# Attention with 16 queries a head: outputs of 15 blocks kept in SBUF and stored by one DMA, and an empty first pass through TensorE's program

## The chip, the core and the metric

The kernel runs on one core of a Trainium2 chip. The metric is the device time of one execution in microseconds (us), as the median of several runs. Shorter is better.

## The reference

```python
B, H, Sq, Skv, Dh = 8, 16, 16, 2048, 256

def reference(q, k, v):
    scale = q.shape[-1] ** -0.5
    scores = jnp.einsum('bhqd,bhkd->bhqk', q, k) * scale
    attn = _softmax(scores, axis=-1)
    return jnp.einsum('bhqk,bhkd->bhqd', attn, v)
```

All is bf16. There are 128 heads (8 x 16), each with 16 queries, 2048 keys and values, and 256 numbers a row. K and V are 134 MB each, q and the output 1 MB each, so the core has to read some 269 MB.

## The kernel before

Eight heads make a block, since 8 heads x 16 queries fill 128 partitions. There are G = 16 blocks (numbers 0 to 15, `last` = 15). Per block 8 MB of K and 8 MB of V are read; a DMA takes 4 MB of K (half a block) or 8 MB of V (a whole block), with 64 to 128 rows of 512 bytes lying one behind the other in each partition. `SL` holds them: two K slots (`KA`, `KB`) and one V window of two slots (`VW`).

What is done with a block:

- VectorE transposes K in place, in 32 x 32 squares (`kt`, line 196).
- TensorE multiplies queries by K into `S_ps` (`qk`, lines 309 and 310).
- VectorE takes the negated maximum (line 220), ScalarE the exponentials and their sums (line 292), VectorE transposes these (lines 229, 231), and both engines copy them into the sparse weights `PTz` (lines 203, 205, 277).
- TensorE multiplies the 128 weight tiles by the 128 V rows of a partition into `O_ps` (`pv`, line 332).
- ScalarE scales the sum by the inverse of the exponentials' sum and writes it as bf16 into the one output buffer `O_fin` (`evac`, line 271).

Each engine has its own program, and semaphores tie them. SyncE (`on_sync`) issues all loads. It waits before each K load until the scores of an earlier block are done (`c_qk`) and before each V load until the V rows that it overwrites have been used (`c_pv`). The V of the last two blocks comes in pieces (`PIECES`: 3 for block 14, 9 for block 15), so that the last ones are small. Behind them SyncE waits for the last eviction (`c_ev`) and stores block 15 (line 156).

ScalarE (`on_scalar`) stores the other 15 blocks from inside its loop: in the round of block g it evicts block g - 1, waits for the write to be done, and issues the store at line 301. Before an eviction it waits on `s_st`, which counts landed stores, since `O_fin` is used again. GpSimd presets the counts (line 161).

TensorE (`on_tensor`) waits for the first weights (`c_qw`), works on the scores of block 0 in small loops, and then has one loop over r from 1 to 16: scores of block r (left out for r = 16), some spare multiplications, and then `pv` for block r - 1, written out as 128 matmuls.

Of the kernel before, what the change touches and what calls it, by code (L numbers as in the profile page):

```python
# [4 lines left out]
ACTF = mybir.ActivationFunctionType  # L5
ALU = mybir.AluOpType
AX = mybir.AxisListType
PE = mybir.EngineType.PE
# [3 lines left out]
BF16 = mybir.dt.bfloat16  # L12
# [3 lines left out]
SPARE = 5  # L16
# [4 lines left out]
def bass_standalone__softmax_full_bidir__sampling_kernel(  # L21
# [16 lines left out]
    ku = k.rearrange("b h s d -> (b h s) d").rearrange("(u p t) d -> u p t d", p=128, t=T)  # L38
    vb = v.rearrange("b h s d -> (b h s) d").rearrange("(g p t) d -> g p t d", p=128, t=2 * T)
    qh = q.rearrange("b h s d -> (b h) (s d)")  # L40
    oh = out.rearrange("b h s d -> (b h s) d").rearrange("(g p) d -> g p d", p=128)

    with ExitStack() as es:
        ec = es.enter_context
# [8 lines left out]

        PTz = ec(nc.sbuf_tensor("PTz", [128, 2, T, 128], BF16))
        mk = ec(nc.sbuf_tensor("mk", [128, 1], F32))
        O_fin = ec(nc.sbuf_tensor("O_fin", [128, D], BF16))
        negm = ec(nc.sbuf_tensor("negm", [128, 1], F32))
        lsum = ec(nc.sbuf_tensor("lsum", [128, 2], F32))
        ltot = ec(nc.sbuf_tensor("ltot", [128, 1], F32))
# [69 lines left out]
        def on_sync(eng):  # L129
            def load_v(w, a, n):  # L130

                eng.wait_ge(c_pv, 8 * w + (a + n + C - 1) // C)
                eng.dma_start(VW[:, a:a + n, :], vb[w, :, a:a + n, :]).then_inc(s_p[w][a] if a else s_v, 16)  # L133

            eng.dma_start(QX, qh).then_inc(s_q, 16)  # L135
            for g, s0, s in ((0, VA, s_k0), (1, KA, s_k)):
                for e in range(2):
                    load_k(eng, g, e, s0 + e, 0, T, s[e])

            for e in range(2):  # L140
                eng.wait_ge(c_qk, 4 * e + 4)
                eng.dma_start(VW[:, T * e:T * e + T, :], vb[0, :, T * e:T * e + T, :]).then_inc(s_v0 if e else s_v, 16)
            with nc.Fori(2, last, engines=[SP]) as j:
                for e in range(2):
                    eng.wait_ge(c_qk, 8 * j + 4 * e - 4)
                    load_k(eng, j, e, KA + e, 0, T, s_k[e])
                load_v(j - 1, 0, 2 * T)
            for e in range(2):
                eng.wait_ge(c_qk, 8 * last + 4 * e - 4)
                load_k(eng, last, e, KA + e, 0, T // 2, s_k[e])  # L150
                load_k(eng, last, e, KA + e, T // 2, T // 2, s_kl[e])
            for w in PIECES:
                for a, n in PIECES[w]:
                    load_v(w, a, n)
            eng.wait_ge(c_ev, G + 1)
            eng.dma_start(oh[last], O_fin[:]).then_inc(s_fin, 16)
            eng.wait_ge(s_fin, 16)

        def on_gpsimd(eng):

            for x, n in ([(c_ev, 1), (c_ri, 2), (c_cp, 1), (c_pv, 8), (s_st, 17)] + [(x, 1) for x in s_kl] +
                         [(x, 1) for w in s_p for x in s_p[w].values()]):
                eng.sem_inc(x, n)
            zero = [PTz[:, e].rearrange("p t c -> p (t c)").bitcast(F32) for e in range(2)]
            eng.memset(zero[0], 0.0).then_inc(c_pool, 1)
            eng.wait_ge(c_qt, 2)
            for n in range(12):

                eng.wait_ge(c_cq if n else c_pool, max(n, 1))
                eng.tensor_copy(*qx(1 + n // 4, n % 4)).then_inc(c_cq, 1)  # L170

            eng.wait_ge(c_qt, 6)
            eng.wait_ge(c_qw, 4)
            eng.wait_ge(c_cq, 12)
            eng.memset(zero[1], 0.0).then_inc(c_pool, 1)
# [81 lines left out]
        def on_scalar(eng):  # L257
            def qwb(src):
                for a in range(4):
                    dv = QW[32 * a:32 * a + 32, :, 16 * a:16 * a + 64, :]  # L260
                    dv = bass.AP(tensor=dv.tensor, offset=QW[32 * a:32 * a + 32, 0, 16 * a, :].offset,
                                 ap=[list(dv.ap[0]), [1024 + 512, 2], [2, 64], [1, 2]])
                    eng.activation(dv, src(a), ACTF.Copy, scale=scale).then_inc(c_qw, 1)  # L263

            def evac(n, st):

                eng.wait_ge(c_pv, 8 * n)
                eng.wait_ge(c_ri, 2 * n)

                eng.wait_ge(s_st, st)  # L270
                eng.activation(O_fin[:], O_ps[:, 0:D], ACTF.Copy, scale=rinv[:, bass.ds(n, 1)]).then_inc(c_ev, 1)  # L271

            def copies(e, rs):
                for r in rs:
                    for x in range(2):
                        dst, src, m = weights(e, r, x)
                        eng.activation(dst, src, ACTF.Copy, scale=m if x else 1.0).then_inc(c_cp, 1)  # L277

            eng.wait_ge(c_qt, 2)
            qwb(lambda a: QXu[0:32, a, 0:2, :, :])  # L280
            eng.wait_ge(c_pool, 2)
            eng.wait_ge(c_qt, 6)
            eng.wait_ge(c_mk, 7)
            with nc.Fori(0, G, engines=[ACT]) as g:
                eng.wait_ge(c_qk, 8 * g + 8)
                qwb(lambda a: QTu[32 * a:32 * a + 32, bass.ds(((g + 1) & 15) * 2, 2), :, :])
                eng.wait_ge(c_mx, g + 1)
                for h in range(2):

                    sv = S_ps[:, 2 * h, :]  # L290
                    sv = bass.AP(tensor=sv.tensor, offset=sv.offset, ap=[list(sv.ap[0]), [32, 32], [1, 2], [2, 16]])
                    eng.activation(P_sb[:, 16 + 1024 * h:16 + 1024 * h + 1024], sv, ACTF.Exp,  # L292
                                   bias=negm[:], scale=1.0, accum_out=lsum[:, h:h + 1]).then_inc(c_ex[h], 1)
                eng.wait_ge(c_pt, 4 * g + 4)
                eng.wait_ge(c_pv, 8 * g + 4)
                copies(0, (0, 1))
                gg = eng.to_reg(g)
                with eng.If_ne(gg, 0):
                    evac(g + 1, 16 * g + 1)
                    eng.wait_ge(c_ev, g + 1)  # L300
                    eng.dma_start(oh[(g + 15) & 15], O_fin[:]).then_inc(s_st, 16)
                copies(1, (0, 1, 2))
            evac(G + 1, 16 * last + 17)

        def on_tensor(eng):
            def mm(dst, w, x, start, stop, load, check=True):
# [8 lines left out]
            def qk(e, cs, slot):  # L315
                for bp in range(8):
                    for c in cs:
                        ins = mm(S_ps[:, c, :], QW[:, e, :, bp], SLk[:, slot, c, bp // 2, bp % 2, :, :],
                                 e == 0 and bp == 0, e == 1 and bp == 7, c == cs[0])
                return ins  # L320
# [13 lines left out]
                    if t % C == C - 1:  # L334
                        ins.then_inc(c_pv, 1)

            eng.wait_ge(c_qw, 4)

            for c in range(4):
                if c == 0:  # L340
                    eng.wait_ge(c_pool, 1)
                mm(S_ps[:, c, :], PTz[:, 0, 0, :], PTz[:, 0, 0:4, :].rearrange("p t m -> p (t m)"), True, False, c == 0, False)
            with nc.Fori(0, 2, engines=[PE]) as e:
                for h in range(2):
                    with nc.Fori(0, 4, engines=[PE]) as b:
                        eng.wait_ge(c_kt, 2 * e + h + 1)
                        for par in range(2):
                            for c in (2 * h, 2 * h + 1):
                                ins = mm(S_ps[:, c, :], QW[:, e, :, 2 * b + par], SLk[:, VA + e, c, b, par, :, :],
                                         False, False, c == 2 * h, False)  # L350
                        if h:
                            ins.then_inc(c_qk, 1)

            with nc.Fori(1, G + 1, engines=[PE]) as r:
                rr = eng.to_reg(r)
                with eng.If_lt(rr, G):
                    for e in range(2):
                        for h in range(2):
                            eng.wait_ge(c_kt, 4 * r + 2 * e + h + 1)
                            if e + h == 0:  # L360
                                eng.wait_ge(c_ex[1], rr)
                            ins = qk(e, (2 * h, 2 * h + 1), KA + e)
                        ins.then_inc(c_qk, 4)

                    mid = eng.to_reg(((r + 14) & 16) + ((r + 1) & 16))
                    with eng.If_eq(mid, 16):
                        with nc.Fori(0, SPARE, engines=[PE]) as x:
                            for _ in range(4):
                                mm(X_ps[:], QW[:, 1, :, 7], QT[:, 0:512], True, True, False)
                lim = {last - 1: eng.to_reg(((r + 1) & 16) + 1), last: eng.to_reg((r & 16) + 1)}  # L370
                eng.wait_ge(c_ev, rr)
                eng.wait_ge(c_cp, 10 * r - 5)
                eng.wait_ge(c_cd, 6 * r - 2)
                eng.wait_ge(s_v, 16 * r)
                pv(lim)

        on_sync(nc.sync)
        on_gpsimd(nc.gpsimd)
# [31 lines left out]
```

## Time and profile before

| | |
|---|---|
| median of 3 runs | 634.5 us (634.5 to 634.57) |
| span of the profiled execution, first to last instruction | 633.1 us |
| HBM read, written | 269.48 MB, 1.05 MB |
| mean rate over the span | 427 GB/s |
| busy: PE, DVE, ACT | 539.1, 444.2, 241.8 us |
| store of one block by ScalarE, issue to landing | 23.5 us (7.9 to 23.9) |
| store of block 15 by SyncE, issue to landing | 1.5 us |

The profile describes one execution. Its own time outside the span isn't listed; 1.4 us lie between its span and the median of the runs. PE is TensorE's matmul, PEld its loading of weights, DVE is VectorE, ACT ScalarE, POOL GpSimd, SP SyncE; a q behind a name means that engine's sequencer. A window is a stretch of the span in us from its start. The DMA share is the mean busy share of the core's 16 DMA engines. Queue q1 carries what SyncE issues, q10 what ScalarE issues; q8 and q14 carry instructions that the engines fetch. In a chain of waits a line gives start, length and what was waited for; in a timeline the bracket at the end gives the idle time before an instruction and what ended it.

### The profile page before, as it was taken

The numbers are of one execution on the slowest core, as the hardware profiler recorded it, in microseconds if no ns is written. First come the engines' busy times: TensorE is split into PE (matmuls) and PEld (weight loads), VectorE is DVE, ScalarE is ACT, GpSimd is POOL, SyncE is SP. The second block draws the span as 40 slices with busy tenths as digits, with TensorE's granted clock in tenths as the row PEclk, the third lists the DMA queues.
The fourth block names the chain that finished last, engine by engine and source line by source line (L and its number), as shares of the span: only waits on it lengthen the run. The fifth ranks groups of instructions, "written<-read, shape, count | busy, mean of one in ns | idle before, by whom it ended". The sixth has DMA issues, their size and how long they took to land.

```text
span 633.1 us, 8100 instructions
## 1 busy us (share of the span) xinstructions
PE 539.1 (85%) x3336; PEld 273.3 (43%) x2561; DVE 444.2 (70%) x285; ACT 241.8 (38%) x309; POOL 21.5 (3%) x18
## 2 busy tenths in 40 slices
PE   1659989889898897989979899797989979899997
PEld 0112824518244272542725336263362724518386
DVE  5989794865948658496575966759567595769750
ACT  1027542622336233352424425244252442623453
POOL 7600000000000000000000000000000000000000
PEclk9998989999898999989999899999998999999999
DMA  8999999999999999999999999999999999999997
GB/s 366 433 433 437 434 443 424 452 411 441 437 428 436 430 433 461 405 459 406 458 413 425 438 427 437 455 404 460 406 462 409 427 437 429 435 420 428 432 427 297
DMA packets 11234, 270.56 MB, mean 427 GB/s; under 512 B 1248, under 2 KB 3552, under 8 KB 3936
## 3 DMA queue, kind: packets, MB, share of 16 engines
q1 hardware_dynamic: 9072, 269.55, 98.8%
q10 hardware_dynamic: 2160, 0.98, 0.5%
q8 instruction: 1, 0.02, 0.0%
q14 instruction: 1, 0.01, 0.0%
HBM read 269.48 MB, written 1.05 MB: 427 GB/s over the span
## 4 chain that ended last, share of the span: by engine, by line
DMA 57%; PE 32%; DVE 6%; issue 4%; SPq 0%; DVEq 0%; ACT 0%
DMA SL<-in_v_dram 45%; PE O_ps L332 30%; DMA SL<-in_k_dram 12%; DVE SL L196 4%; PE S_ps L309 1%; PE S_ps L310 1%; DVE PTz L203 0%; DVE PTb L231 0%; DVE negm L220 0%; DVE PTz L205 0%; DVE PTa L229 0%; SPq L127 0%; SPq L133 0%; ACT O_fin L271 0%; SPq L135 0%
## 5 line engine op out<-in xcount | busy, mean ns | idle before, releaser
L196 DVE STREAM_TRANSPOSE SL<-SL 128x4096 f32<-128x4096 f32 x64 | 282.3, 4433 | 81.7 <-DMA SL<-in_k_dram 80.8
L309 PE MATMUL S_ps<-SL,QW 128*128 128x512 bf16 (+1 forms) x512 | 206.3, 403 | 68.5 <-DVE SL L196 58.9
L332 PEld LDWEIGHTS O_ps<-SL,PTz 128*128 128x128 bf16 x2048 | 198.8, 98 | 103.0 <-DMA SL<-in_v_dram 79.2
L332 PE MATMUL O_ps<-SL,PTz 128*128 128x256 bf16 x2048 | 226.7, 273 | 13.5 <-DMA SL<-in_v_dram 12.4
L310 PE MATMUL S_ps<-SL,QW 128*128 128x512 bf16 (+1 forms) x512 | 204.8, 400 | 0.0
L309 PEld LDWEIGHTS S_ps<-SL,QW 128*128 128x128 bf16 (+1 forms) x512 | 74.3, 145 | 244.6 <-issue 155.2
L263 ACT ACTIVATE QW<-QT 32x256 bf16 x64 | 26.9, 420 | 202.5 <-PE S_ps L310 201.3
L277 ACT ACTIVATE PTz<-PTa 16x1024 bf16<-16x1024 bf16 x32 | 33.8, 1056 | 112.0 <-PE O_ps L332 100.2
L220 DVE TENSOR_REDUCE negm<-S_ps 128x1 f32<-128x2048 f32 x16 | 36.6, 2289 | 55.1 <-PE S_ps L310 55.1
L310 PE MATMUL X_ps<-QT,QW 128*128 128x512 bf16 x260 | 58.2, 379 | 0.0
L277 ACT ACTIVATE PTz<-PTb 16x1024 bf16<-16x1024 bf16 x48 | 50.6, 1055 | 10.9 <-ACT O_fin L271 10.1
L229 DVE STREAM_TRANSPOSE PTa<-P_sb 128x1024 bf16<-128x1024 bf16 x32 | 39.2, 1224 | 21.9 <-ACT P_sb L292 21.9
L277 ACT ACTIVATE PTz<-PTa,mk 32x1024 bf16<-32x1024 bf16 x48 | 54.3, 1130 | 0.0
L231 DVE STREAM_TRANSPOSE PTb<-P_sb 128x1024 bf16<-128x1024 bf16 (+1 forms) x32 | 39.0, 1218 | 0.0
L292 ACT ACTIVATE P_sb<-S_ps,negm 128x1024 bf16<-128x1024 f32 x32 | 35.4, 1110 | 5.9 <-DVE negm L220 5.9
L277 ACT ACTIVATE PTz<-PTb,mk 32x1024 bf16<-32x1024 bf16 x32 | 36.2, 1132 | 0.0
L271 ACT ACTIVATE O_fin<-O_ps,rinv 128x256 bf16<-128x256 f32 x16 | 7.6, 474 | 51.5 <-PE O_ps L332 51.5
L203 DVE TENSOR_SCALAR PTz<-PTb,mk 32x1024 bf16<-32x1024 bf16 x32 | 15.2, 476 | 0.0
L205 DVE COPY PTz<-PTa 16x1024 bf16<-16x1024 bf16 x32 | 13.5, 422 | 1.6 <-PE O_ps L332 0.6
L170 POOL COPY QT<-PTz 32x1024 bf16<-32x1024 bf16 x12 | 14.3, 1192 | 3.2 <-DVE PTz L187 2.5
L205 DVE COPY PTz<-PTb 16x1024 bf16<-16x1024 bf16 x16 | 6.8, 424 | 3.4 <-PE O_ps L332 3.0
L309 PE MATMUL S_ps<-PTz 128*128 128x512 bf16 x1 | 0.6, 610 | 9.9 <-ACT QW L263 9.9
(21 smaller groups left out, 38.8 us busy)
## 6 DMA issues: line engine op xcount, KB each, us to landing
SL<-in_k_dram SPq DMA_DIRECT2D x30, 4096.0 KB, 24.3
SL<-in_v_dram SPq DMA_DIRECT2D x2, 4096.0 KB, 21.9
SL<-in_k_dram SPq DMA_DIRECT2D x4, 2048.0 KB, 21.1
SL<-in_v_dram SPq DMA_DIRECT2D x2, 2048.0 KB, 18.7
SL<-in_v_dram SPq DMA_DIRECT2D x1, 3584.0 KB, 21.0
SL<-in_v_dram SPq DMA_DIRECT2D x1, 2560.0 KB, 23.6
SL<-in_v_dram SPq DMA_DIRECT2D x1, 1792.0 KB, 11.0
SL<-in_v_dram SPq DMA_DIRECT2D x1, 1472.0 KB, 12.6
```

The lines of the kernel that those rows point to most:

```text
L196: eng.transpose(x, x).then_inc(c_kt, 1)
L203: ins = eng.tensor_scalar(out=dst, in0=src, scalar1=m, scalar2=None, op0=ALU.mult)
L205: ins = eng.tensor_copy(dst, src)
L220: eng.tensor_reduce(out=negm[:], in_=S_ps[:].rearrange("p c n -> p (c n)"), axis=AX.X, op=ALU.max, negate=True).then_inc(c_mx, 1)
L229: eng.transpose(fa[:, 1024 * h:1024 * h + 1024], P_sb[:, 16 + 1024 * h:16 + 1024 * h + 1024]).then_inc(c_pt, 1)
L231: eng.transpose(fb[:, 1024 * h:1024 * h + n], P_sb[:, 1024 * h:1024 * h + n]).then_inc(c_pt, 1)
L263: eng.activation(dv, src(a), ACTF.Copy, scale=scale).then_inc(c_qw, 1)
L277: eng.activation(dst, src, ACTF.Copy, scale=m if x else 1.0).then_inc(c_cp, 1)
L292: eng.activation(P_sb[:, 16 + 1024 * h:16 + 1024 * h + 1024], sv, ACTF.Exp, bias=negm[:], scale=1.0, accum_out=lsum[:, h:h + 1]).then_inc( ...
L309: return eng.matmul(dst, w, x, start=start, stop=stop, skip_group_check=not check)
L310: return eng.add_instruction(mybir.InstMatmult(name=nc.get_next_instruction_name(), engine=PE, start_tensor_calc=start, stop_tensor_calc=stop,
L332: ins = eng.matmul(O_ps[:, 0:D], PTz[:, t // T, t % T, :], VW[:, t, :], start=(t == 0), stop=(t == 2 * T - 1))
```

## The change

`O_fin` becomes `O_all` with one place for each block. ScalarE's evictions write into it one after the other, with no wait for a store, and no store is issued in the loop. Behind its last V piece SyncE waits for the eviction of block 14 and issues one DMA for blocks 0 to 14 (128 partitions x 15 rows of 512 bytes). Block 15 is stored by ScalarE right behind its eviction. SyncE then waits for both.

TensorE's whole program is put into a loop of two rounds, under a condition that is false in the first: in round 0 it branches over everything to the end of the loop and back, in round 1 it works as before.

In ScalarE's loop this stands before, from the branch that leaves out round 0 to the first copies of the block's second half (`L` is the line; ISA rows are waits with a register):

```order
L298 COMPARE_AND_BRANCH
L267 REGISTER_ALU
L268 REGISTER_ALU
L270 ISA
L271 ISA
L271 ACTIVATE O_fin<-O_ps,rinv 128x256
L301 REGISTER_ALU x2
L301 ISA
L301 DMA out_dram<-O_fin 128x256
L298 UNCONDITIONAL_BRANCH
L277 ACTIVATE PTz<-PTb 16x64x16
L277 ACTIVATE PTz<-PTa,mk 32x64x16
```

And in the changed kernel, with the end of its program:

```order
L299 COMPARE_AND_BRANCH
L269 REGISTER_ALU
L270 REGISTER_ALU
L271 ISA
L271 ACTIVATE O_all<-O_ps,rinv 128x256
L299 UNCONDITIONAL_BRANCH
L278 ACTIVATE PTz<-PTb 16x64x16
L278 ACTIVATE PTz<-PTa,mk 32x64x16
...
L271 ACTIVATE O_all<-O_ps,rinv 128x256
L304 DMA out_dram<-O_all 128x256
```

The wait for an earlier store (L270), the wait for the eviction's write and the DMA behind it are gone from the loop; one DMA stands behind the last eviction.

The end of SyncE's program, the last V pieces (elements per partition in the size) and what follows, first before and then in the changed kernel:

```order
L133 DMA SL<-in_v_dram 128x2048
L133 DMA SL<-in_v_dram 128x1280
L133 DMA SL<-in_v_dram 128x768
L133 DMA SL<-in_v_dram 128x512
L156 DMA out_dram<-O_fin 128x256
```

```order
L134 DMA SL<-in_v_dram 128x2048
L134 DMA SL<-in_v_dram 128x1280
L134 DMA SL<-in_v_dram 128x768
L134 DMA SL<-in_v_dram 128x512
L157 DMA out_dram<-O_all 128x15x256
```

The order of the loads is the same; the DMA behind them moves 15 blocks in place of one.

The start and the end of TensorE's program in the changed kernel (before, it began with the L310 matmul, there L309, and ended with the branch of the r loop, here L358):

```order
L338 UNCONDITIONAL_BRANCH
L340 COMPARE_AND_BRANCH
L310 MATMUL S_ps<-PTz 128x512
L311 MATMUL S_ps<-PTz 128x512 x3
...
L333 MATMUL O_ps<-SL,PTz 128x256 x64
L358 REGISTER_ALU
L358 COMPARE_AND_BRANCH
L340 UNCONDITIONAL_BRANCH
L338 REGISTER_ALU
L338 COMPARE_AND_BRANCH
```

In the first round the L340 branch goes to the L338 rows at the far end, and the last branch returns to the start.

The diff; TensorE's part is cut, its lines are only moved to the right:

```diff
--- before.py
+++ after.py
@@ -38,7 +38,7 @@
     ku = k.rearrange("b h s d -> (b h s) d").rearrange("(u p t) d -> u p t d", p=128, t=T)
     vb = v.rearrange("b h s d -> (b h s) d").rearrange("(g p t) d -> g p t d", p=128, t=2 * T)
     qh = q.rearrange("b h s d -> (b h) (s d)")
-    oh = out.rearrange("b h s d -> (b h s) d").rearrange("(g p) d -> g p d", p=128)
+    oh = out.rearrange("b h s d -> (b h s) d").rearrange("(g p) d -> p g d", p=128)
 
     with ExitStack() as es:
         ec = es.enter_context
@@ -53,7 +53,8 @@
 
         PTz = ec(nc.sbuf_tensor("PTz", [128, 2, T, 128], BF16))
         mk = ec(nc.sbuf_tensor("mk", [128, 1], F32))
-        O_fin = ec(nc.sbuf_tensor("O_fin", [128, D], BF16))
+
+        O_all = ec(nc.sbuf_tensor("O_all", [128, G + 2, D], BF16))
         negm = ec(nc.sbuf_tensor("negm", [128, 1], F32))
         lsum = ec(nc.sbuf_tensor("lsum", [128, 2], F32))
         ltot = ec(nc.sbuf_tensor("ltot", [128, 1], F32))
@@ -152,13 +153,14 @@
             for w in PIECES:
                 for a, n in PIECES[w]:
                     load_v(w, a, n)
-            eng.wait_ge(c_ev, G + 1)
-            eng.dma_start(oh[last], O_fin[:]).then_inc(s_fin, 16)
+            eng.wait_ge(c_ev, G)
+            eng.dma_start(oh[:, 0:last, :], O_all[:, 2:G + 1, :]).then_inc(s_st, 16)
             eng.wait_ge(s_fin, 16)
+            eng.wait_ge(s_st, 16)
 
         def on_gpsimd(eng):
 
-            for x, n in ([(c_ev, 1), (c_ri, 2), (c_cp, 1), (c_pv, 8), (s_st, 17)] + [(x, 1) for x in s_kl] +
+            for x, n in ([(c_ev, 1), (c_ri, 2), (c_cp, 1), (c_pv, 8)] + [(x, 1) for x in s_kl] +
                          [(x, 1) for w in s_p for x in s_p[w].values()]):
                 eng.sem_inc(x, n)
             zero = [PTz[:, e].rearrange("p t c -> p (t c)").bitcast(F32) for e in range(2)]
@@ -262,13 +264,12 @@
                                  ap=[list(dv.ap[0]), [1024 + 512, 2], [2, 64], [1, 2]])
                     eng.activation(dv, src(a), ACTF.Copy, scale=scale).then_inc(c_qw, 1)
 
-            def evac(n, st):
+            def evac(n):
 
                 eng.wait_ge(c_pv, 8 * n)
                 eng.wait_ge(c_ri, 2 * n)
-
-                eng.wait_ge(s_st, st)
-                eng.activation(O_fin[:], O_ps[:, 0:D], ACTF.Copy, scale=rinv[:, bass.ds(n, 1)]).then_inc(c_ev, 1)
+                eng.activation(O_all[:, bass.ds(n, 1), :].rearrange("p o d -> p (o d)"), O_ps[:, 0:D], ACTF.Copy,
+                               scale=rinv[:, bass.ds(n, 1)]).then_inc(c_ev, 1)
 
             def copies(e, rs):
                 for r in rs:
@@ -296,11 +297,11 @@
                 copies(0, (0, 1))
                 gg = eng.to_reg(g)
                 with eng.If_ne(gg, 0):
-                    evac(g + 1, 16 * g + 1)
-                    eng.wait_ge(c_ev, g + 1)
-                    eng.dma_start(oh[(g + 15) & 15], O_fin[:]).then_inc(s_st, 16)
+                    evac(g + 1)
                 copies(1, (0, 1, 2))
-            evac(G + 1, 16 * last + 17)
+            evac(G + 1)
+            eng.wait_ge(c_ev, G + 1)
+            eng.dma_start(oh[:, last, :], O_all[:, G + 1, :]).then_inc(s_fin, 16)
 
         def on_tensor(eng):
             def mm(dst, w, x, start, stop, load, check=True):
@@ -334,45 +335,48 @@
                     if t % C == C - 1:
                         ins.then_inc(c_pv, 1)
 
-            eng.wait_ge(c_qw, 4)
-
-            for c in range(4):
...
-            with nc.Fori(0, 2, engines=[PE]) as e:
...
-            with nc.Fori(1, G + 1, engines=[PE]) as r:
...
-                eng.wait_ge(s_v, 16 * r)
-                pv(lim)
+            with nc.Fori(0, 2, engines=[PE]) as z:
+                zz = eng.to_reg(z)
+                with eng.If_ne(zz, 0):
+                    eng.wait_ge(c_qw, 4)
+
+                    for c in range(4):
...
+                    with nc.Fori(0, 2, engines=[PE]) as e:
...
+                    with nc.Fori(1, G + 1, engines=[PE]) as r:
...
+                        eng.wait_ge(s_v, 16 * r)
+                        pv(lim)
```

More of the change, by code (lines that the diff above doesn't have):

```diff
@@ L335, in pv @@
                         ins.then_inc(c_pv, 1)
-            eng.wait_ge(c_qw, 4)
-            for c in range(4):
-                if c == 0:
-                    eng.wait_ge(c_pool, 1)
-                mm(S_ps[:, c, :], PTz[:, 0, 0, :], PTz[:, 0, 0:4, :].rearrange("p t m -> p (t m)"), True, False, c == 0, False)
-            with nc.Fori(0, 2, engines=[PE]) as e:
[L344 to L352, printed above, removed]
@@ L354, in on_tensor @@
-            with nc.Fori(1, G + 1, engines=[PE]) as r:
-                rr = eng.to_reg(r)
-                with eng.If_lt(rr, G):
-                    for e in range(2):
-                        for h in range(2):
[L359 to L373, printed above, removed]
-                eng.wait_ge(s_v, 16 * r)
-                pv(lim)
+            with nc.Fori(0, 2, engines=[PE]) as z:
[3 more added lines that the diff above has]
+                    for c in range(4):
+                        if c == 0:
+                            eng.wait_ge(c_pool, 1)
+                        mm(S_ps[:, c, :], PTz[:, 0, 0, :], PTz[:, 0, 0:4, :].rearrange("p t m -> p (t m)"), True, False, c == 0, False)
+                    with nc.Fori(0, 2, engines=[PE]) as e:
+                        for h in range(2):
+                            with nc.Fori(0, 4, engines=[PE]) as b:
+                                eng.wait_ge(c_kt, 2 * e + h + 1)
+                                for par in range(2):
+                                    for c in (2 * h, 2 * h + 1):
+                                        ins = mm(S_ps[:, c, :], QW[:, e, :, 2 * b + par], SLk[:, VA + e, c, b, par, :, :],
+                                                 False, False, c == 2 * h, False)
+                                if h:
+                                    ins.then_inc(c_qk, 1)
+                    with nc.Fori(1, G + 1, engines=[PE]) as r:
+                        rr = eng.to_reg(r)
+                        with eng.If_lt(rr, G):
+                            for e in range(2):
+                                for h in range(2):
+                                    eng.wait_ge(c_kt, 4 * r + 2 * e + h + 1)
+                                    if e + h == 0:
+                                        eng.wait_ge(c_ex[1], rr)
+                                    ins = qk(e, (2 * h, 2 * h + 1), KA + e)
+                                ins.then_inc(c_qk, 4)
+                            mid = eng.to_reg(((r + 14) & 16) + ((r + 1) & 16))
+                            with eng.If_eq(mid, 16):
+                                with nc.Fori(0, SPARE, engines=[PE]) as x:
+                                    for _ in range(4):
+                                        mm(X_ps[:], QW[:, 1, :, 7], QT[:, 0:512], True, True, False)
+                        lim = {last - 1: eng.to_reg(((r + 1) & 16) + 1), last: eng.to_reg((r & 16) + 1)}
+                        eng.wait_ge(c_ev, rr)
+                        eng.wait_ge(c_cp, 10 * r - 5)
+                        eng.wait_ge(c_cd, 6 * r - 2)
+                        eng.wait_ge(s_v, 16 * r)
+                        pv(lim)
```

## The prediction

> **What bounds the kernel now.** I first read the part on DMA queues, then a table of stretches one block long.
>
> ```profile
> q1 hardware_dynamic: 9072, 269.55, 98.8%
> q10 hardware_dynamic: 2160, 0.98, 0.5%
> q8 instruction: 1, 0.02, 0.0%
> q14 instruction: 1, 0.01, 0.0%
> ```
>
> The loads (q1, SyncE) and ScalarE's 15 stores (q10) together fill 98.8 + 0.5 = 99.3% of what 16 DMA engines have in 633.1 us. The stores are 15 x 64 KB.
>
> ```profile
> core 0: us, PE busy (x) PEld busy (x) DVE busy (x) ACT busy (x) POOL busy (x), PEclk, DMA share, GB/s
> 235.20:274.10 38.90, 33.38 (x213) 17.00 (x160) 27.24 (x18) 14.92 (x19) 0.00 (x0) 1.00 1.00 433
> 429.85:468.80 38.95, 33.47 (x213) 17.07 (x161) 27.32 (x18) 14.93 (x19) 0.00 (x0) 1.00 1.00 432
> ```
>
> In a block of about 38.9 us the DMA share is 1.00, while TensorE is busy for 33.4 us and VectorE for 27.3. The chain of waits shows how a block is tied to the next:
>
> ```profile
> 429.85 24.57 DMA SL<-in_v_dram
> 454.46 14.16 PE O_ps L332 x128
> 468.78 24.56 DMA SL<-in_v_dram
> ```
>
> A V load of 8 MB takes 24.6 us from its issue. At 432 GB/s its bytes need 8.39 MB / 432 GB/s = 19.4 us, so it first stands some 5 us behind the K loads already queued. That backlog of 5 us is why the engines never run dry, and why the chain's alternation of PE and DMA is no latency bound: if the queue got shorter by x, the wait in it would shrink by x. The bound is the engines' total work; whatever is taken out of the stream shortens the block by as much.
>
> At the end I read the chain again, then the timelines of ScalarE and SyncE:
>
> ```profile
> 600.20 7.00 PE O_ps L332 x64
> 607.22 12.46 DMA SL<-in_v_dram
> 619.72 11.29 PE O_ps L332 x100
> 631.04 0.47 ACT O_fin L271
> ...
> 614.46 0.47 ACT L271 ACTIVATE O_fin<-O_ps,rinv 128x256 bf16<-128x256 f32 x1 [1.57 <-PE O_ps L332]
> 615.22 0.34 ACTq L301 DMA_DIRECT2D out_dram<-O_fin  x1
> 615.61 1.06 ACT L277 ACTIVATE PTz<-PTb 16x1024 bf16<-16x1024 bf16 x1 [0.67 <-ACT O_fin L271]
> 620.80 1.13 ACT L277 ACTIVATE PTz<-PTa,mk 32x1024 bf16<-32x1024 bf16 x1
> ...
> 607.22 8.74 SPq L133 DMA_DIRECT2D SL<-in_v_dram  x8
> 631.54 0.34 SPq L156 DMA_DIRECT2D out_dram<-O_fin  x1
> ```
>
> The second piece of the last V lands at 619.7 us; from there TensorE runs its last 100 matmuls with hardly a gap (113 ns each), then come one eviction and one store. How the DMA engines drain shows in the GB/s rows of three windows, 40 slices each (628.5 to 630.5, 629.5 to 631.5, 631.4 to 633.1):
>
> ```profile
> GB/s 205 184 195 103 123 51 102 72 102 0 82 31 62 21 51 51 51 51 20 72 31 31 21 20 20 20 20 41 20 0 0 0 0 0 0 0 0 0 0 0
> GB/s 31 31 21 20 20 20 20 41 20 0 0 0 0 0 0 0 0 0 0 0 0 0 0 0 0 0 0 0 0 0 0 0 0 0 0 0 0 0 0 0
> GB/s 0 0 0 0 0 0 0 0 0 0 0 0 0 0 0 0 0 0 0 0 0 0 0 96 205 301 313 253 217 109 48 0 0 0 0 0 0 0 0 0
> out_dram<-O_fin SPq DMA_DIRECT2D x1, 64.0 KB, 1.5
> ```
>
> Most engines have nothing left by about 628.9. Then some 20 to 50 GB/s goes on until 629.95: with 432/16 = 27 GB/s for an engine, that is two engines, at last one, about 1 us behind the rest. The final 64 KB moves alone in 8 or 9 slices of 42.5 ns, 0.36 us; its last bytes are at 632.7, 0.4 us before the span ends at 633.1.
>
> **The change, part by part.** The sum is made against the span, 633.1 us; the median of the runs is 634.5, so 1.4 us lie around the span, and I leave them as they are.
>
> *Fifteen stores leave the stream.* By the queue's share, one costs each engine 0.5% x 633.1 / 15 = 0.21 us. A stretch with one store gives nearly the same:
>
> ```profile
> q1 hardware_dynamic: 453, 4.13, 97.6%
> q10 hardware_dynamic: 144, 0.07, 2.3%
> ```
>
> (615 to 625 us: 2.3% of 10 us = 0.23 us.) From below, by bytes alone: 64 KB / 432 GB/s = 0.15. I take 0.21, since loads and stores add up to the full share. Ahead of the last V piece that sets the end stand the stores of blocks 0 to 13: 14 x 0.21 = **2.9 us** (2.1 to 3.2). For the draining of the queue it is all 15, 3.15 us (2.3 to 3.4).
>
> *ScalarE's part.* Its wait for an earlier store, and 0.67 us of idle time between eviction and next copy, go. The copies end at 620.80 + 1.13 = 621.9, and TensorE needs them at its 65th matmul, 619.72 + 36 x 0.113 = 623.8. So nothing is gained there; the cover is 1.9 us at the end of the program, and more in a block where TensorE waits for V. The final store moves from SyncE's queue to ScalarE's; either issue takes 0.34 us by the rows above. Nothing stands behind it on ScalarE. A bigger buffer and one semaphore preset less on GpSimd cost nothing on a path.
>
> *The one big store.* SyncE reaches it after its last V issue, at 607.22 + 8.74 = 615.96 minus what is saved. The wait for the eviction of block 14 (614.93) is over by then. If issuing 15 blocks took 15 times 0.34 us = 5.1 us, it would end at 621, still before the loads drain; nothing but SyncE's two last waits is queued behind it. Its packets stand behind all V pieces on q1, so V isn't delayed. No row shows 960 KB stored at one go. From below: 15 x 0.21 = 3.15 us. From above: each block as its own 0.36 us, 5.4 us. I take 15 x 0.22 = 3.3, because the packets are the same 128 x 512 B per block that cost 0.21 to 0.23 under full load.
>
> *The empty first pass of TensorE.* It adds a branch out and one back near the start.
>
> ```profile
> 9.92 0.61 PE L309 MATMUL S_ps<-PTz 128*128 128x512 bf16 x1 [9.92 <-ACT QW L263]
> 64.55 14.13 PE L332 MATMUL O_ps<-SL,PTz 128*128 128x256 bf16 x128
> q14 instruction: 1, 0.01, 2.1%
> q8 instruction: 1, 0.02, 6.7%
> ```
>
> TensorE waits for ScalarE until 9.92, which hides the pass. The two instruction fetches of the span fall in the windows 65 to 66 (q14) and 67 to 68 (q8), just after TensorE first enters its P x V code at 64.55; that run has no gap (14.13 us against 14.16 later), so no stall is to be won. But each fetch is one packet on one DMA engine: 6.7% of 16 x 1 us is 1.07 us for q8, 2.1% gives 0.34 us for q14. In a stream without slack that engine stays behind for good, and each load lands with its last engine. The 1 us by which one or two engines are late at the end is just this size. Fetched near time 0, before K streams, the packet would cost little. If q8 is TensorE's and its engine the last one, up to 1.0 us is won; if another engine is as late for another reason, nothing is. I take **0.5 us**.
>
> [...]
>
> *The sum.* TensorE's way to the end: 633.1 - 2.9 - 0.5 = 629.7. The queue's way: the last engine drains at 629.95 - 3.15 - 0.5 = 626.3, the big store takes 3.3, its landing 0.4: 630.0. So the two ends almost meet, the big store lies just ahead of the final 64 KB, and the later one counts: span 630.0, time 630.0 + 1.4 = **631.4 us**.
>
> **Rivals.** About 0.2%, 1.27 us, is what a measurement of this kernel can tell from no change.
>
> *The pass brings nothing.* [...] For it: q14's fetch, by whichever engine, isn't touched if that is not TensorE. Then the queue's way is 626.8 + 3.3 + 0.4 = 630.5, time 631.9.
>
> *The big store sets the end.* At 5.4 us it ends at 626.3 + 5.4 + 0.4 = 632.1, time 633.5. For it: the final store alone shows 0.36 us for 64 KB. Against: of these 0.36 the first and last slices are ramps (96, 48 GB/s) that a long store has once.
>
> [...]
>
> *The stores weren't paid for.* If their packets fit into gaps, removing them wins nothing: queue's way 629.95 + 3.3 + 0.4 = 633.65, time 635.0. Against: a share of 1.00.
>
> **How the numbers follow.** Forecast 0.42, pass without effect 0.25, big store at the end 0.15, receipts 0.11, stores free 0.07. Lowest bound of the forecast: TensorE's way 633.1 - 3.2 - 1.0 = 628.9, the queue's way 629.95 - 3.4 - 1.0 + 3.15 + 0.4 = 629.1, with 1.4 some 630.5; a little below that lies room for the shares' rounding, 630.0. Upward I go past the 633.5 of the slower big store to 634.2, which leaves out the receipts and some of the free stores, about 2 in 10. Faster by over 0.2% (under 633.2): 0.42 + 0.25 + half of 0.15 = 0.75. Same: the other half and most of the free stores, 0.13. Slower: 0.12.
>
> **What would show it.** Right: q10 with 144 packets, a block of 38.7 us at share 1.00, the last V eviction some 3 to 3.5 us earlier, q8's packet in the first 3 us, no single engine 1 us late in the drain, the big store at about 300 GB/s and over as the final 64 KB starts. Wrong: blocks still at 38.9 us, a q8 packet still near 65 us, a gap between SyncE's last wait and ScalarE's store, or a drain in which 512 B packets move at under 150 GB/s.

## The result, and the profile after

| | before | changed | ratio |
|---|---|---|---|
| median of 7 runs | 634.5 us | 632.53 us | 0.9968 [0.9958, 0.9978] |
| span of the profiled execution | 633.1 us | 631.3 us | |

One of the seven runs before took 3079.66 us and is left aside; the other six lie between 634.44 and 634.64. The change makes the kernel 2.0 us faster. 631.4 us was forecast, with a range of 630.0 to 634.2: the direction is right, and the gain is about two thirds of the 3.1 us that were worked out.

The DMA queues of the changed kernel (packets, MB, share of 16 engines' span):

```profile
q1 hardware_dynamic: 10864, 270.47, 99.8%
q10 hardware_dynamic: 144, 0.07, 0.0%
q8 instruction: 1, 0.02, 0.0%
q14 instruction: 1, 0.01, 0.0%
```

ScalarE's queue q10 carries only block 15; the other 15 blocks' bytes are on q1 now. To see what a store had cost, compare the same two pieces of the chain of waits nine blocks apart, first before, then in the changed kernel (start, length, what):

```profile
142.99 14.16 PE O_ps L332 x128
...
493.39 14.16 PE O_ps L332 x128
```

```profile
142.91 14.16 PE O_ps L333 x128
...
491.90 14.16 PE O_ps L333 x128
```

Nine blocks take 350.40 us before and 348.99 after: 38.93 and 38.78 us a block. A 64 KB store was worth 0.157 us of the block, not 0.21. The table of stretches, of the changed kernel, shows that the engines are as full as before (the last two columns are the DMA share and GB/s):

```profile
196.00:234.78 38.78, 34.76 (x208) 17.12 (x161) 27.29 (x18) 14.80 (x19) 0.00 (x0) 0.96 1.00 433
428.66:467.45 38.79, 33.16 (x208) 17.07 (x161) 27.28 (x18) 14.80 (x19) 0.00 (x0) 1.00 1.00 433
```

The end of the changed kernel, from its chain and the timelines of SyncE and ScalarE:

```profile
617.73 11.22 PE O_ps L333 x100
628.97 0.47 ACT O_all L271
...
614.22 0.43 SPq L157 DMA_DIRECT2D out_dram<-O_all  x1
629.48 0.37 ACTq L304 DMA_DIRECT2D out_dram<-O_all  x1
```

TensorE's last run of 100 matmuls starts 2.0 us earlier (619.72 before) and takes nearly as long (11.22 us against 11.29). The last eviction stands at 628.97 against 631.04, so up to there 2.07 us are won. The span is only 1.8 us shorter: 0.27 us are given back behind the eviction. The big store took 0.43 us to issue. The DMA engines' rate from 626 to 631.3 us (40 slices of 0.13 us) and the time to landing of the big store and the final one:

```profile
GB/s 367 352 410 367 344 356 379 348 379 359 359 340 340 363 348 344 352 344 356 348 344 348 348 344 352 309 236 182 162 151 143 128 124 267 251 77 50 0 0 0
out_dram<-O_all SPq DMA_DIRECT2D x1, 960.0 KB, 16.9
...
out_dram<-O_all ACTq DMA_DIRECT2D x1, 64.0 KB, 1.8
```

From about 628 on, where the loads are gone (the run without the big store, below, shows them until 627.9), the big store alone moves at 344 to 356 GB/s. Then the rate falls from 352 to 124 GB/s, as if the engines finished one by one, until the final 64 KB comes (the rise to 267) while the big store is still running. The big store lands at 614.22 + 16.9 = 631.1, the final one at 629.48 + 1.8 = 631.3, so the two ends all but meet. The final store takes 1.8 us, against 1.5 for the one that SyncE issued alone before.

Last, the instruction fetch of TensorE and what it hits. The rows of the changed kernel are the share of q8 in 3.5 to 5.5 us, the landing of q, VectorE's transposition of q, and SyncE's issue of block 1's V:

```profile
q8 instruction: 1, 0.02, 2.9%
...
PTz<-in_q_dram SPq DMA_DIRECT2D x1, 1024.0 KB, 6.1
...
6.84 2.31 DVE L189 STREAM_TRANSPOSE PTz<-PTz 128x2048 f32<-128x2048 f32 x1 [4.38 <-DMA PTz<-in_q_dram]
...
80.67 0.33 SPq L134 DMA_DIRECT2D SL<-in_v_dram  x1
```

Before:

```profile
PTz<-in_q_dram SPq DMA_DIRECT2D x1, 1024.0 KB, 5.0
...
5.75 2.31 DVE L187 STREAM_TRANSPOSE PTz<-PTz 128x2048 f32<-128x2048 f32 x1 [3.29 <-DMA PTz<-in_q_dram]
...
78.86 0.33 SPq L133 DMA_DIRECT2D SL<-in_v_dram  x1
```

The pass does move the fetch, from about 68 us to between 3.5 and 5.5 us, and 2.9% of 16 x 2 us is 0.93 us of one engine. But q is being loaded there: q lands 1.1 us later, the first transposition starts 1.1 us later, and block 1's V is issued 1.8 us later (some of that isn't the pass's: the kernel with the stores alone, below, issues it at 79.44).

### The profile page after: what moved, and what is told of

Same layout as the page of the kernel before. It is cut to its first block, busy times and chain, and to the rows that moved or that the text cites. A ratio compares the mean times of both kernels' runs of the same rounds, so it can differ in the third digit from the quotient of the medians.

```text
span 631.3 us, 7952 instructions
## 1 busy us (share of the span) xinstructions
PE 534.5 (85%) x3271; PEld 273.4 (43%) x2561; DVE 444.2 (70%) x285; ACT 239.9 (38%) x309; POOL 21.5 (3%) x18
## 4 chain that ended last, share of the span: by engine, by line
DMA 53%; PE 35%; DVE 7%; issue 4%; ACT 0%; SPq 0%; DVEq 0%
DMA SL<-in_v_dram 44%; PE O_ps L333 30%; DMA SL<-in_k_dram 8%; DVE SL L198 5%; PE S_ps L310 2%; PE S_ps L311 2%; DVE negm L222 1%; PE X_ps L311 1%; DVE PTz L205 1%; DVE PTz L207 0%; DVE PTb L233 0%; DVE PTa L231 0%; ACT P_sb L293 0%; SPq L128 0%; SPq L134 0%
## 5 line engine op out<-in xcount | busy, mean ns | idle before, releaser
L310 PE MATMUL S_ps<-SL,QW 128*128 128x512 bf16 (+1 forms) x512 | 205.8, 402 | 69.6 <-DVE SL L198 59.5
L310 PEld LDWEIGHTS S_ps<-SL,QW 128*128 128x128 bf16 (+1 forms) x512 | 74.4, 145 | 244.6 <-issue 155.5
L311 PE MATMUL X_ps<-QT,QW 128*128 128x512 bf16 x195 | 52.7, 379 | 3.5
L271 ACT ACTIVATE O_all<-O_ps,rinv 128x256 f32 (+1 forms) x16 | 7.6, 473 | 51.4 <-PE O_ps L333 51.4
L310 PE MATMUL S_ps<-PTz 128*128 128x512 bf16 x1 | 0.6, 609 | 11.0 <-ACT QW L265 11.0
## 6 DMA issues: line engine op xcount, KB each, us to landing
SL<-in_v_dram SPq DMA_DIRECT2D x1, 1792.0 KB, 10.9
```

The costliest lines, as they stand in the source:

```text
L310: return eng.matmul(dst, w, x, start=start, stop=stop, skip_group_check=not check)
L311: return eng.add_instruction(mybir.InstMatmult(name=nc.get_next_instruction_name(), engine=PE, start_tensor_calc=start, stop_tensor_calc=stop,
```

## The experiments

**The stores alone.** TensorE's program stays as before.

```diff
-            with nc.Fori(0, 2, engines=[PE]) as z:
-                zz = eng.to_reg(z)
-                with eng.If_ne(zz, 0):
-                    eng.wait_ge(c_qw, 4)
+            eng.wait_ge(c_qw, 4)
...
```

> The change without TensorE's empty first pass. Theory A (all of the gain comes from the 15 stores that left the stream, 14 x 0.147 us ahead of the last V piece, and the pass only moves a fetch from 68 us to 4 us, where it delays one DMA engine by the same 1 us): within 0.4 us of the changed kernel's 632.5, span 631.3, the instruction packet of q8 back in the window 66 to 69. Theory B (the pass brings a part, 0.5 us as forecast): 633.0 or more.

Measured: 632.5 us (632.42 to 632.56), ratio 0.9969 [0.9957, 0.9981], span 631.2. TensorE's fetch in the window 66 to 68, the issue of block 1's V, and the last eviction:

```profile
q8 instruction: 1, 0.02, 3.3%
...
79.44 0.33 SPq L134 DMA_DIRECT2D SL<-in_v_dram  x1
...
628.83 0.47 ACT O_all L271
```

The eviction is 2.21 us earlier than before (631.04), which is 14 x 0.157 = 2.2: the stores are the whole gain. It is even 0.14 us earlier than with the pass. Theory A holds, B falls.

**The pass alone.** The other half of the change, on the kernel before.

```diff
-            eng.wait_ge(c_qw, 4)
+            with nc.Fori(0, 2, engines=[PE]) as z:
+                zz = eng.to_reg(z)
+                with eng.If_ne(zz, 0):
+                    eng.wait_ge(c_qw, 4)
...
```

> The kernel before with nothing but the empty first pass. Theory A: 634.5, no change beyond 0.4 us, q8's packet at 4 us. Theory B: 634.0 or less.

Measured: 634.54 us (634.33 to 635.36) beside 634.48 for the kernel before, ratio 1.0002 [0.9993, 1.0011]. No gain. Of its 11 runs three lay at 635.2 to 635.4, the profiled one (span 634.0) among them. In that one the stretch from 78 to 103 us is slower than before; the second row is before:

```profile
78.00:103.00 25.00, 20.16 (x99) 6.53 (x52) 20.14 (x11) 10.43 (x14) 0.00 (x0) 1.00 0.99 414
```

```profile
78.00:103.00 25.00, 21.37 (x91) 5.06 (x36) 19.64 (x12) 10.18 (x14) 0.00 (x0) 0.93 0.98 425
```

414 against 425 GB/s over 25 us is 0.6 us. The engines weren't idle there: the DMA share is 0.99 against 0.98. Block 1's V is issued late in this run (80.60), but the changed kernel issues it as late (80.67) without the loss. Block 1's `pv` in this run, before, and in the changed kernel:

```profile
105.07 14.16 PE O_ps L332 x128
...
104.05 14.16 PE O_ps L332 x128
...
104.19 14.10 PE O_ps L333 x128
```

The loss is there by block 1; what makes it in some runs and not in others stays open.

**The change without the big store.** Blocks 0 to 14 are left out of the output.

```diff
-            eng.dma_start(oh[:, 0:last, :], O_all[:, 2:G + 1, :]).then_inc(s_st, 16)
             eng.wait_ge(s_fin, 16)
-            eng.wait_ge(s_st, 16)
```

> The changed kernel without the store of blocks 0 to 14, which are left out of the output. Theory A (the big store ends at 630.7 and shares the engines with the final 64 KB, which takes 0.56 us there and 0.36 us alone): 0.2 to 0.3 us faster than the changed kernel, 632.3. Theory C (the big store costs nothing at the end): same time. Theory D (it sets the end): 1 us or more faster.

Measured: 632.38 us (632.23 to 632.6, and one run at 633.35), ratio 0.997 [0.9958, 0.9981], span 631.0. The DMA engines' rate from 626 to 631 us (40 slices of 0.125 us), and the final store alone:

```profile
GB/s 381 332 230 131 111 94 86 62 49 41 25 25 25 25 16 0 0 0 0 0 0 0 0 0 0 0 0 0 0 0 0 0 0 0 152 283 90 0 0 0
...
out_dram<-O_all ACTq DMA_DIRECT2D x1, 64.0 KB, 1.6
```

The median is 0.15 us less than the changed kernel's, somewhat under what A said, but the runs overlap (632.42 to 632.75 there); the landing took 1.6 us in place of 1.8. With intervals of about 0.7 us to either side of each ratio, C (no cost) isn't excluded by the times, only made less likely by the landing. D falls: without the big store the end comes 0.15 us earlier and not 1 us.

This run also shows how the loads drain by themselves, with the pass in place. The rate falls under 200 GB/s at 626.4, and what is left goes on until 627.9, at the end at one engine's rate (25 GB/s and less, beside 432 / 16 = 27). In the kernel before, it fell under 200 at 628.6 and went on until 629.95. So the last load comes 2.1 us earlier, which is about the stores' sum, and the tail is as long as before although TensorE's fetch ran in the window 3.5 to 5.5 us.

**Stores twice.** The kernel before with all blocks kept, and each of blocks 0 to 13 stored again one round later.

```diff
...
-                    eng.dma_start(oh[(g + 15) & 15], O_fin[:]).then_inc(s_st, 16)
+                    eng.dma_start(oh[(g + 15) & 15], O_all[:, bass.ds(g + 1, 1), :].rearrange("p o d -> p (o d)")).then_inc(s_st, 16)
+                    with eng.If_ne(gg, 1):
+                        eng.dma_start(oh[(g + 14) & 15], O_all[:, bass.ds(g, 1), :].rearrange("p o d -> p (o d)")).then_inc(s_st, 16)
...
```

> The kernel before, with all blocks kept in SBUF and each of blocks 0 to 13 stored a second time one round later, so 14 more stores of 64 KB in the stream. Theory A (a store costs the stream its bytes, 64 KB / 432 GB/s = 0.15 us): 13 or 14 x 0.147 = 2 us more than before, 636.5. Theory E (it costs the 0.21 us that its packets take on each engine): 2.9 us more, 637.4.

Measured: 636.84 us, ratio 1.0037 [1.0023, 1.0051], span 635.1. Its queue, the same piece of the chain six blocks apart, and its last eviction:

```profile
q10 hardware_dynamic: 4176, 1.90, 1.0%
...
143.00 14.16 PE O_ps L335 x128
...
377.48 14.16 PE O_ps L335 x128
...
633.04 0.47 ACT O_all L271
```

29 stores in place of 15, twice the share. A block takes 234.48 / 6 = 39.08 us, 0.15 more than before (38.93). The eviction comes 2.00 us later than before (631.04). The last extra store is issued when the last V piece that counts is already on its way, so 13 or 14 stores made this: 0.154 or 0.143 us a store. In the span A's 2.0 us is met. The time rose by 2.36 us, since the runs' time outside the span was some 1.6 us in place of 1.3; what that is was not tried. 636.84 is nearer to A's 636.5 than to E's 637.4.

**Loads held back, with and without the pass.** SyncE waits for GpSimd's first memset before its first K load. One kernel has this on the changed kernel, the other on the kernel with the stores alone.

```diff
+            eng.wait_ge(c_pool, 1)
             for g, s0, s in ((0, VA, s_k0), (1, KA, s_k)):
```

> The changed kernel with SyncE waiting for GpSimd's first memset (done at about 5.1 us) before its first K load, so that q8's fetch at 4.0 to 5.0 us falls on idle DMA engines. The stream starts some 3.5 us later, which both held kernels pay. Theory F (one engine's 1 us for the fetch is on the path to the end wherever the stream runs): 0.7 to 1.0 us faster than the held kernel without the pass, with no engine 1 us late as the loads drain. Theory G (the late engine costs nothing at the end, or another engine is as late): the same time as the held kernel without the pass, within 0.3 us.

> The kernel with the stores changed but without the pass, and with SyncE held in the same way. q8's fetch falls at 66 to 73 us, in the stream. Theories F and G both: 632.5 + 3.5 = 636.0 us, one engine 1 us late as the loads drain. They differ in the other held kernel: F has it at 635.0 to 635.3, G at 636.0.

Measured: with the pass 634.37 us (634.04 to 634.58), ratio 0.9998 [0.9989, 1.0007]; without it 634.84 us (634.68 to 635.0), ratio 1.0005 [0.9996, 1.0014]. The late start costs them 1.8 and 2.3 us, less than the 3.5 us expected: K's issue waits until 5.5 us, but the engines have q to load in any case, which lands 4.8 us (without the pass) to 6.1 us (with it) behind its issue at 0.75. With the pass: the fetch in 3.5 to 5.5 us, the first K issue, and the last matmuls in the chain:

```profile
q8 instruction: 1, 0.02, 2.9%
...
5.53 1.86 SPq L128 DMA_DIRECT2D SL<-in_k_dram  x4
...
619.53 11.19 PE O_ps L334 x100
```

Without it (the fetch in 67 to 70.5 us):

```profile
q8 instruction: 1, 0.02, 1.9%
...
619.87 11.19 PE O_ps L334 x100
```

The fetch lies in the window that ends at 5.5 us and K is issued from 5.53 on, and now the pass wins 0.34 us in the chain and 0.47 us in the time; the two sets of runs don't overlap. That lies between F (0.7 to 1.0) and G (under 0.3). So the fetch has a price in the stream: a third to nearly a half of the 1.07 us that its packet takes. The drains (627 to 633 us, 40 slices of 0.15 us; with the pass, then without) bear on why it isn't all of it:

```profile
GB/s 423 413 403 393 383 376 393 321 386 365 341 331 345 372 328 362 348 345 358 338 345 365 328 358 352 341 358 338 287 167 68 48 38 20 184 246 45 20 0 0
```

```profile
GB/s 410 430 362 403 369 355 379 369 379 376 321 389 331 358 355 341 372 341 345 352 345 348 355 338 358 345 341 345 294 201 123 79 44 41 44 44 143 277 75 20
```

An engine in the big store moves about 350 / 16 = 22 GB/s. Without the pass two engines' rate (41 to 44) goes on up to the final 64 KB. With it the tail is shorter, but it ends on one engine (20), still some 0.5 us behind the steep fall. So one engine is late even where TensorE's fetch no longer hits the stream. The q14 fetch falls into the stream in both kernels and is a candidate; a kernel without it wasn't tried, so why the price is not the whole 1.07 us stays open.

## Why the prediction was right or wrong

The direction and the main mechanism were right, but the forecast was 1.1 us too low. Two terms were too large, the stores by 0.7 us and the pass by 0.5 us; the stated range was wide enough to hold both errors.

- *The bound: right.* The DMA engines' total work sets the block. Taking the stores out shortened each block (38.93 us to 38.78), putting more in lengthened it (to 39.08), and in the changed kernel share and rate stayed at 1.00 and 433 GB/s.
- *Fifteen stores leave the stream: mechanism right, size wrong.* 0.21 us a store was chosen from the queue's share over 0.15 from bytes at the stream's rate. Measured by the length of a block: 0.157 with the stores out and 0.15 with them doubled, so 14 x 0.157 = 2.2 us in place of 2.9. That is the value from bytes, 0.15, which the prediction had as its lower one. The recorded time of a store's packets (0.21 to 0.23 us) was no measure of what it took from the stream; "loads and stores add up to the full share" was no reason for the higher value.
- *ScalarE's part: as forecast.* In the changed kernel ScalarE no longer waits behind the eviction: the group of copies that stood idle for 10.9 us over the whole program, 10.1 of them behind `O_fin`, stands idle for 0.8. The last eviction of the kernel with the stores alone moved by the stores' sum, so no further gain is seen.
- *The big store: mechanism right, size a little high.* SyncE had issued it at 614.7, long before the loads drained, and it ran at about 350 GB/s: at that rate 960 KB take 2.8 us, less than the 3.15 that was to be its lower bound. The queue's way comes out with it: the last load at 627.9, 2.8 for the store and 0.4 for its landing give 631.1, where it landed. The rival at 5.4 us falls. The "receipts" of the chances (0.11) are shown by no run: 960 KB went at about 350 GB/s. The two ends did nearly meet; the final 64 KB may have paid some 0.15 us for it (632.53 against 632.38), which the runs don't separate from nothing.
- *The empty first pass: the failed step.* "Fetched near time 0, before K streams, the packet would cost little" was the premise of the 0.5 us. The packet came between 3.5 and 5.5 us, while q was still being loaded with K right behind. So no time is won at the end: 634.54 against 634.48 alone, 632.53 against 632.5 on top of the stores. The sign "no single engine 1 us late in the drain" failed with it, as the run without the big store shows. That it is the engine of the fetch, now late from the first block instead of the second, fits this and q's landing 1.1 us later, but is inferred: the rows don't name the engine. With the loads held until 5.5 us, the 0.5 us did appear (0.47), but holding them costs about 2 us, so the price of the fetch was real and only its new place no better. The rival "the pass brings nothing" (0.25) was the true case, though the fetch did move, and wasn't repeated: the changed kernel has one q8 packet in its span.
- *The sum with measured terms, made afterwards:* 634.5 - 2.2 (stores) - 0 (pass) + 0.15 (the final store beside the big one, not clear of the runs' spread) = 632.45, measured 632.53.

No version that beats the changed kernel came out of the runs. The stores alone give the same time with the simpler TensorE program.

## What to carry to other kernels

In a kernel like this one, whose DMA engines are full throughout, a small store among large loads cost about its bytes at the stream's rate (64 KB at 432 GB/s are 0.15 us; 0.157 and 0.15 us of a block were measured), so price it from the change of a block's length or from bytes, not from its packets' recorded times (0.21 to 0.23 us). Put behind the last load, such stores were nearly free here: 632.53 us with them, 632.38 without, the big store landing at 631.1 and the last result at 631.3. Moving the fetch won nothing where it ran during q's load with K right behind (634.54 us against 634.48), and 0.47 us where K's loads were held back until 5.5 us, so look in the trace for when a packet really runs, not for when the program asks for it.

## What the runs showed of the hardware

- The issue of a DMA took 0.43 us for 1920 rows of 512 bytes and 0.34 to 0.37 us for 128 rows.
- Rows of 512 bytes were stored at 344 to 356 GB/s once no loads ran, against 432 GB/s for loads in rows of 32 to 64 KB.
- Nothing stands ahead of the jump in TensorE's program, but the packet of its fetch (q8, 0.02 MB) ran only in the window 3.5 to 5.5 us, even where K was held back until 5.53 us and only q was loading.
